# Retention of ten tiles ahead of the main loop, a fixed order of the first loads, and weights joined in PSUM

## The chip, the core and the metric

The program runs on one core of one Trainium2 chip. The core has a matrix engine (PE, with its weight loads shown apart as PEld), a vector engine (DVE), a scalar engine (ACT), a general engine (POOL) and a queue engine (SP) that issues DMAs. Matrix results go to PSUM, which has eight banks of 128 x 512 float32 here; everything else lies in SBUF. The metric is the time of one execution on the chip in microseconds (us): for the kernel before, the median of three runs is 748.28 us (748.04 to 749.37).

## What is computed

Retention over 2304 tokens with 8 heads of 64, and then two MLPs. The weights arrive as float64.

```python
scores = scale * q @ k.T                    # per head, 4 batches of 576 tokens
attn = (scores * gamma ** (i - j))[i >= j] @ v
h = x @ w_in                                # first MLP, 512 -> 1024
solu = h * softmax(h)
ln = (solu - mean) / sqrt(var + 1e-6) * g_ln
x = ln @ w_out                              # 1024 -> 512
h = x @ w_in2                               # second MLP, 512 -> 2048
g = where(h >= 1, h, where(h <= -1, 0, (h + 1) ** 2 / 4))
out = g @ w_out2                            # 2048 -> 512
```

## The kernel before

The tokens are 18 tiles of 128. Retention is recurrent: each tile makes its scores (`ret_scores`, step S: eight matmuls at L116, their product with the decays on DVE at L125, and on POOL the scaling of q, L129, and of k, L132), and its output (`ret_out`, step O: state times q at L144, scores times v at L150, the new state's product at L168, and its addition to the state on DVE at L175 or L181). The output is split into two float32r parts, high and low, on ACT and DVE (L74, L75); every product of the MLPs is three float32r matmuls of such parts.

A weight comes as pairs of 32-bit words and is turned into float32 by `decode`: ACT rescales the high words (L193) and the low words (L194), DVE shifts (L195), POOL adds as integers (L196), and DVE joins the sign (L197, a SCALAR_TENSOR_TENSOR with both its inputs in SBUF). Then ACT writes the high part and DVE or POOL subtracts (L75, for the first MLP's second weight L221 with L223, L224 or L227). Steps A are the four pieces of the first weight `w_in1` (two decodes each), steps B the eight pieces of `w_out1` (one decode each), and `prep_w2` makes the 16 pairs of the second MLP.

What stands ahead of the main loop is written in the string START: L loads a tile of q, k and v, C and G load constants, H is half of a tile's hidden matmuls (L243), N its norm. A step in small letters takes another engine for part of its work. Within START a scheduler places the instructions of all engines, the DMA issues on SP too, by its own estimates; START's steps are only its priorities. After START the matrix engine follows the written order; the other engines are still scheduled. In the main loop, for j = 1 to 8 and a = 2 j, tiles a and a + 1 of the first MLP are worked on, and retention of tiles a + 6 and a + 7 (`LEAD` is 6), until tile 17. With START's S0 to S7 and O0 to O7, the loop begins retention at tile 8.

Loads of q, k and v go through two buffers each (pool `raw`), so the load of a tile waits for the output step of the tile two before it. PSUM has four tags of two banks: `sc` (scores), `o` (retention), `h` (hidden of the first MLP, later projections) and `tr` (transposes). In the second MLP the first block's halves `hidden(0, c)` alternate between `sc` and `tr` for c of 4 and more, and 12 of the 16 weight pairs are prepared while that block runs, after the first MLP's SBUF is free.

Of the kernel before, what the change touches and what calls it, by code (L numbers as in the profile page):

```python
# [24 lines left out]
P = 128  # L25
# [10 lines left out]
START = """  # L36
C1 C0 L0 A0 G0 a1 L1 L2 s0 S1 L3 a2 L4 S2 G1 O0 S3 B0 o1 A3 B1 B2 O2 b3 O3 b4 H0 H1 S4 L5 O4 S5 O5 b5 N0 L6 B6 H2 S6 O6 H3 L7 N1 S7 O7 L8 B7
"""


def shape_constants():
    """The retention's decays, from the shapes alone. Heads are 2 c + e. Within a tile, gamma^(i - j) / sqrt(D)
    from key j to query i >= j; gamma^(i + 1) / sqrt(D) from the row before the tile; gamma^(P - 1 - j) to its
    last row; gamma^P across it."""
    gamma = 1.0 - 2.0 ** (-5.0 - np.arange(H, dtype=np.float64))
    g = gamma.reshape(KD, 2).T
    i = np.arange(P)
# [9 lines left out]
def net(ctx: ExitStack, tc: tile.TileContext, qk_t, kv, w_in1, w_out1, g_ln, w_in2, w_out2, inside, before, after, across, out):  # L57
# [27 lines left out]

# [1 line left out]
    in_sb = at.tile([P, 2, KD, P], F32, name="in_sb", bufs=1)  # L87
# [48 lines left out]
    def ret_out(t, alt=False):  # L136
# [10 lines left out]
        for c in range(KD):  # L147
            for e in range(2):
# [33 lines left out]

# [5 lines left out]
    def decode(st, sp=None):  # L188
# [16 lines left out]
    def prep_w_in1(i, alt=False):  # L205
# [25 lines left out]

# [1 line left out]
    lnT, hps, es = {}, {}, {}  # L233
# [16 lines left out]
    def mlp1_norm(t, alt=False):  # L250
# [78 lines left out]

    def prep_w2(pool, i, sp=None, n0=0):  # L330
# [3 lines left out]
        split(hi.rearrange("p c f -> p (c f)"), lo.rearrange("p c f -> p (c f)"), decode(st, sp))  # L334
# [8 lines left out]
    def split_x2(b):  # L343
# [45 lines left out]

# [1 line left out]
    gs = {}  # L391
# [4 lines left out]
    order = ExitStack()  # L396
    for step in START.split():
        if step[0].islower():
            start[step[0].upper()](int(step[1:]), True)
        else:  # L400
            start[step[0]](int(step[1:]))
    order.enter_context(tc.manual_schedule(engines={nc.tensor.engine}))
# [12 lines left out]
    for j in range(1, NT // 2):  # L415
# [24 lines left out]
        mlp1_hidden(a + 1, 0)  # L440
# [106 lines left out]
```

## Time and profile before

| | |
|---|---|
| median of three runs | 748.28 us |
| the profiled execution, span from first to last instruction | 751.0 us |
| PE busy | 720.1 us (96%) |
| DVE busy | 435.4 us (58%) |
| ACT busy | 285.4 us (38%) |
| POOL busy | 169.8 us (23%) |
| mean granted PE clock | 0.978 |

The trace gives no time of the profiled execution other than its span, so that is its own time here; it is 2.7 us above the median of the runs. Busy time of an engine is the time in which it had an instruction under way; a matmul at a lower granted clock is busy for longer, so busy PE time is not the amount of its work.

### The profile page before, as it was taken

The page shows a single profiled execution, that of the slowest core. Times are in us where ns is not written, and L with a number is a line of the kernel's source. Part 1 is how long each engine was busy: PE and PEld are TensorE (multiplying, and loading weights), DVE is VectorE, ACT ScalarE, POOL GpSimd, SP SyncE. Part 2 cuts the span into 40 slices and gives each one's busy share as a digit, 9 for nine tenths or more (in the row PEclk, how much of TensorE's full clock was granted, in tenths as well). Part 3 has the DMA queues.
Part 4 walks back from the last instruction along what each step waited for, and adds up shares of the span by engine and source line. Part 5 has one row for each costly group of instructions (what it writes and reads, how often), then busy time and mean ns, then how long its engine had stood idle before and what let it go on. Part 6 is the DMA issues. An engine that isn't in the chain of part 4 may idle for free.

```text
span 751.0 us, 10316 instructions
## 1 busy us (share of the span) xinstructions
PE 720.1 (96%) x4096; PEld 606.4 (81%) x4096; DVE 435.4 (58%) x777; ACT 285.4 (38%) x555; POOL 169.8 (23%) x154
## 2 busy tenths in 40 slices
PE   4789999999999999989798999999999999999998
PEld 4678788989888899879676888888888888888896
DVE  4796986574746847685998543344443353434443
ACT  3533663232424635575754322222321242223222
POOL 2785843221211402155654000000000000000000
PEclk9895999999999999999989999999999999999999
DMA  8653543111200301036500010000100001000100
GB/s 342 260 195 115 192 149 110 57 59 55 86 29 1 113 1 57 29 113 211 180 29 28 1 56 1 1 0 1 57 0 1 1 17 40 0 1 1 57 1 28
DMA packets 15183, 50.21 MB, mean 67 GB/s; under 512 B 1952, under 2 KB 2464, under 8 KB 14624
## 3 DMA queue, kind: packets, MB, share of 16 engines
q1 hardware_dynamic: 14848, 49.30, 18.3%
q8 instruction: 32, 0.52, 0.3%
q10 hardware_dynamic: 288, 0.26, 0.1%
q14 instruction: 15, 0.12, 0.1%
HBM read 44.84 MB, written 4.72 MB: 66 GB/s over the span
## 4 chain that ended last, share of the span: by engine, by line
PE 77%; DVE 12%; issue 3%; ACT 3%; POOL 3%; DMA 2%; SPq 0%; POOLq 0%; DVEq 0%; ACTq 0%
PE po L377 23%; PE h L358 23%; PE hp L243 11%; PE px L319 10%; DVE y L197 3%; PE sc L116 2%; DVE y L195 2%; PE po L150 2%; PE pst L168 2%; POOL y L196 2%; DMA st<-in_w_in 2%; PE tp L290 2%; PE po L144 1%; ACT y L193 1%; DVE r L362 1%
## 5 line engine op out<-in xcount | busy, mean ns | idle before, releaser
L377 PE MATMUL po<-wo,gh 128*128 128x512 f32 x576 | 194.1, 398 | 2.7 <-ACT gh L74 2.7
L358 PE MATMUL h<-xsh,wi 128*128 128x512 f32 (+1 forms) x640 | 195.8, 372 | 0.0
L362 DVE SCALAR_TENSOR_TENSOR r<-r 128x512 f32<-128x512 f32 (+1 forms) x80 | 55.6, 695 | 145.6 <-ACT r L361 145.4
L358 PEld LDWEIGHTS h<-xsh,wi 128*128 128x128 f32 x640 | 117.1, 188 | 23.3
L377 PEld LDWEIGHTS po<-wo,gh 128*128 128x128 f32 x576 | 109.2, 190 | 28.9 <-POOL y L196 2.5
L358 PE MATMUL h<-xsl,wi 128*128 128x512 f32 (+1 forms) x320 | 119.0, 372 | 0.0
L377 PE MATMUL po<-wo,gl 128*128 128x512 f32 x288 | 115.1, 400 | 3.8 <-DVE gl L75 3.8
L361 ACT ACTIVATE r<-h 128x512 f32<-128x512 f32 (+1 forms) x80 | 44.3, 554 | 150.6 <-PE h L358 150.1
L243 PE MATMUL hp<-wi1h,x 128*128 128x512 f32 x288 | 91.5, 399 | 0.0
L196 POOL TENSOR_TENSOR y<-y,st 128x512 int32<-128x512 int32 x48 | 67.9, 1418 | 78.0 <-DVE y L195 69.4
L74 ACT ACTIVATE gh<-r 128x512 fp32r<-128x512 f32 (+1 forms) x80 | 47.1, 589 | 95.6 <-DVE r L365 95.6
L319 PE MATMUL px<-lnh,wo1l 128*128 128x256 f32 x288 | 80.8, 281 | 0.0
L319 PE MATMUL px<-lnh,wo1h 128*128 128x256 f32 x288 | 79.7, 277 | 0.0
L319 PE MATMUL px<-lnl,wo1h 128*128 128x256 f32 x288 | 79.7, 277 | 0.0
L75 DVE TENSOR_TENSOR gl<-r,gh 128x512 fp32r<-128x512 f32 (+1 forms) x80 | 55.0, 687 | 42.0 <-ACT gh L74 41.7
L358 PEld LDWEIGHTS h<-xsl,wi 128*128 128x128 f32 x320 | 60.4, 189 | 12.0
L377 PEld LDWEIGHTS po<-wo,gl 128*128 128x128 f32 x288 | 54.6, 190 | 17.5 <-DVE gl L75 5.5
L243 PEld LDWEIGHTS hp<-wi1h,x 128*128 128x128 f32 x288 | 55.3, 192 | 11.9
L243 PE MATMUL hp<-wi1l,x 128*128 128x512 f32 x144 | 60.4, 419 | 3.4 <-DVE wi1l L75 3.3
L197 DVE SCALAR_TENSOR_TENSOR y<-st,y 128x512 uint32<-128x512 uint32 x48 | 49.1, 1024 | 11.1 <-POOL y L196 11.1
L319 PEld LDWEIGHTS px<-lnh,wo1l 128*128 128x128 f32 x288 | 54.1, 188 | 1.3 <-DVE wo1l L227 0.2
L319 PEld LDWEIGHTS px<-lnl,wo1h 128*128 128x128 f32 x288 | 54.1, 188 | 0.2
(73 smaller groups left out, 920.8 us busy)
## 6 DMA issues: line engine op xcount, KB each, us to landing
st<-in_w_out SPq DMA_DIRECT2D x24, 512.0 KB, 3.5
qk<-in_qk_t SPq DMA_DIRECT2D x18, 512.0 KB, 4.3
kv<-in_kv SPq DMA_DIRECT2D x18, 512.0 KB, 3.2
st<-in_w_in SPq DMA_DIRECT2D x16, 512.0 KB, 3.3
st<-in_w_in SPq DMA_DIRECT2D x4, 1024.0 KB, 9.5
out<-osb SPq DMA_DIRECT2D x8, 512.0 KB, 2.8
in_sb<-in_inside SPq DMA_DIRECT2D x2, 256.0 KB, 2.8
bef_sb<-in_before SPq DMA_DIRECT2D x1, 256.0 KB, 8.4
```

The lines of the kernel that those rows point to most:

```text
L74: nc.scalar.activation(hi, src, AF.Copy)
L75: eng.tensor_tensor(out=lo, in0=src, in1=hi.bitcast(F32), op=ALU.subtract)
L116: nc.tensor.matmul(sc[e][:, c, :], qk[rows, 1, c, :], qk[rows, 0, c, :], start=True, stop=True)
L150: nc.tensor.matmul(po[rows, c, :], kv_[:, 1, 2 * c + e, :], probs[t, e][:, c, :], start=(c == 0 and n_in == 0), stop=(c == KD - 1), skip_g ...
L196: nc.gpsimd.tensor_tensor(out=y.bitcast(I32), in0=y.bitcast(I32), in1=lo.bitcast(I32), op=ALU.add)
L197: nc.vector.scalar_tensor_tensor(out=y, in0=hi, scalar=0x80000000, in1=y, op0=ALU.bitwise_and, op1=ALU.bitwise_or)
L243: nc.tensor.matmul(hp, a[:, kk, :], w[:, fs], start=(n == 0), stop=(n == 3 * KD - 1))
L319: nc.tensor.matmul(px[:, mm, :], w[:, ms], a[:, f, :], start=(n == 0), stop=(n == 3 * C1 - 1))
L358: nc.tensor.matmul(hp[:, :n], w[:, kk, :], a[:, :n], start=(i == 0), stop=(i == 3 * KD - 1))
L361: nc.scalar.activation(r[:, :n], hp[:, :n], AF.Relu, bias=0.5, scale=0.5)
L362: nc.vector.scalar_tensor_tensor(out=r[:, :n], in0=r[:, :n], scalar=1.0, in1=r[:, :n], op0=ALU.min, op1=ALU.mult)
L377: nc.tensor.matmul(po[i], a[:, ts_], w, start=(c == 0 and j == 0), stop=(c == C2 - 1 and j == 2))
```

## The change

- START holds the retention of tiles 0 to 9 and loads up to tile 11; in the loop, retention begins at tile 10 (`more = 10 <= ra < NT`), and loads go one tile further ahead. `LEAD` stays 6. The split parts of tiles 0 to 3 lie in buffers of the second MLP's inputs, which are free then.
- SP keeps the order in which START's steps are written (`manual_schedule` on the SP engine). L0 is the first step.
- In `decode`, for the first MLP's weights, ACT writes the rescaled high words to PSUM, and DVE's shift and join read them there; the joined weight stays in PSUM, or goes to SBUF where POOL subtracts. In the second MLP the rescaled words stay in SBUF, and the join writes its result to PSUM. Both splits there run on DVE; before, those of the second weight of a pair ran on POOL.
- Weights take banks of the tags `tr` and `h` (START), `o` (second MLP's pairs 0 to 2) and `tr` (the rest). `hidden(0, c)` of the first block has `sc` alone.
- In the steps B in small letters ACT multiplies by `g` in place of POOL.

```diff
-C1 C0 L0 A0 G0 a1 L1 L2 s0 S1 L3 a2 L4 S2 G1 O0 S3 B0 o1 A3 B1 B2 O2 b3 O3 b4 H0 H1 S4 L5 O4 S5 O5 b5 N0 L6 B6 H2 S6 O6 H3 L7 N1 S7 O7 L8 B7
+L0 C1 C0 G0 L1 s0 A0 G1 O0 S1 L2 o1 A1 L3 S2 o2 A2 L4 S3 A3 O3 L5 S4 B0 O4 L6 S5 b1 O5 L7 B2 S6 O6 H0 H1 L8 b3 S7 O7 N0 L9 B4 S8 O8 b5 H2 H3 L10 S9 O9 N1 B6 b7 L11
...
-        slot = t % LEAD
-        if slot < 2:
+        slot = (t - 4) % LEAD
+        if t < 4:
+            xh, xl = (slab.tile([P, KD, P], F32R, tag=f"xs{w}", name="x1", bufs=4) for w in "hl")
+        elif slot < 2:
...
+    def decode(st, tag, sp=None, sb=False):
...
+        if sp:
+            y = sp.tile([P, 512], U32, tag="y", name="y", bufs=2 if sp is stage else 4)
...
+            w = ps.tile([P, 512], U32, tag=tag, name="w")
+            nc.vector.scalar_tensor_tensor(
+                out=w, in0=hi, scalar=0x80000000, in1=y, op0=ALU.bitwise_and, op1=ALU.bitwise_or
+            )
+            return w.bitcast(F32)
+        w = ps.tile([P, 512], U32, tag=tag, name="w")
+        y = stage.tile([P, 512], U32, tag="y", name="y", bufs=2)
+        nc.scalar.activation(w.bitcast(F32), hi.bitcast(F32), AF.Copy, scale=2.0**-112)
         nc.scalar.activation(lo.bitcast(I32), lo, AF.Copy, scale=2.0**-29)
-        nc.vector.tensor_scalar(y, y, 3, None, op0=ALU.logical_shift_left)
+        nc.vector.tensor_scalar(y, w, 3, None, op0=ALU.logical_shift_left)
         nc.gpsimd.tensor_tensor(out=y.bitcast(I32), in0=y.bitcast(I32), in1=lo.bitcast(I32), op=ALU.add)
+        r = y if sb else w
         nc.vector.scalar_tensor_tensor(
-            out=y, in0=hi, scalar=0x80000000, in1=y, op0=ALU.bitwise_and, op1=ALU.bitwise_or
+            out=r, in0=w, scalar=0x80000000, in1=y, op0=ALU.bitwise_and, op1=ALU.bitwise_or
         )
-        return y.bitcast(F32)
+        return r.bitcast(F32)
...
-            split(hi[:, fs], lo[:, fs], decode(st[:, fs, :]), nc.gpsimd if j and not alt else nc.vector)
+            w = decode(st[:, fs, :], "h" if j else "tr", sb=j)
+            split(hi[:, fs], lo[:, fs], w, nc.gpsimd if j else nc.vector)
...
-        split(hi, lo, decode(st, sp), nc.gpsimd)
+        split(hi, lo, decode(st, tag, sp or stage))
...
-        hp = ps.tile([P, BLK], F32, tag=tag or ("tr" if c % 2 else "sc"), name="h2")
+        hp = ps.tile([P, BLK], F32, tag=tag or ("tr" if c % 2 and b else "sc"), name="h2")
...
+    with tc.manual_schedule(engines={nc.sync.engine}):
+        for step in START.split():
+            start[step[0].upper()](int(step[1:]), *[True] * step[0].islower())
...
-        more = ra < NT
+        more = 10 <= ra < NT
```

How the instructions stand now is shown at three places. The first is SP's queue at the very start. In the kernel before it reads as follows (qk, kv: a tile's q and k, k and v; st: words of a weight; in_sb, aft_sb, bef_sb, acr_sb, g_sb: constants; numbers are buffers).

```order
L96 DMA in_sb_96<-in_inside 128x512 x2
L105 DMA qk_104<-in_qk_t 128x1024
L106 DMA kv_105<-in_kv 128x1024
L207 DMA st_108<-in_w_in1 128x2048
L100 DMA aft_sb_98<-in_after 128x8
L100 DMA bef_sb_97<-in_before 128x512
L207 DMA st_130<-in_w_in1 128x2048
L105 DMA qk_150<-in_qk_t 128x1024
L106 DMA kv_151<-in_kv 128x1024
L207 DMA st_194<-in_w_in1 128x2048
```

In the changed kernel the same place reads so.

```order
L105 DMA qk_104<-in_qk_t 128x1024
L106 DMA kv_105<-in_kv 128x1024
L96 DMA in_sb_96<-in_inside 128x512 x2
L100 DMA aft_sb_98<-in_after 128x8
L100 DMA bef_sb_97<-in_before 128x512
L105 DMA qk_112<-in_qk_t 128x1024
L106 DMA kv_113<-in_kv 128x1024
L222 DMA st_131<-in_w_in1 128x2048
L100 DMA acr_sb_99<-in_across 128x4
L100 DMA g_sb_93<-in_g_ln 128x8
L105 DMA qk_192<-in_qk_t 128x1024
L106 DMA kv_193<-in_kv 128x1024
```

Tile 0's q and k went from the third transfer to the first, and both first tiles stand ahead of the first piece of `w_in1`; of that weight's pieces, three stood among the first twelve issues before and one does now.

The second place is PE where it meets the first hidden matmuls (hp; wi1l, wi1h: the low and high parts of `w_in1`, x1: the split output of tile 0). In the kernel before they follow the scores of tile 1.

```order
L116 MATMUL sc0_173<-qk_150 128x128
L116 MATMUL sc1_174<-qk_150 128x128
L243 MATMUL hp_436<-wi1l0_111,x1_246 128x512
L243 MATMUL hp_436<-wi1h0_110,x1_247 128x512
L243 MATMUL hp_436<-wi1h0_110,x1_246 128x512
L144 MATMUL po_286<-qs_187,state_100 128x128 x4
```

In the changed kernel they follow the scores of tile 7, behind the state product of that tile (po_543).

```order
L150 MATMUL po_483<-p1_464,kv_387 64x128
L116 MATMUL sc1_527<-qk_448 128x128 x4
L144 MATMUL po_543<-qs_540,state_100 128x128 x4
L259 MATMUL hp_569<-wi1l0_134,x1_164 128x512
L259 MATMUL hp_569<-wi1h0_133,x1_165 128x512
L259 MATMUL hp_569<-wi1h0_133,x1_164 128x512
L259 MATMUL hp_569<-wi1l1_227,x1_164 128x512
```

Before, hidden matmuls stood between the retention steps from tile 1 on, a weight piece at a time; now 110 rows of retention alone, of tiles 0 to 7, stand ahead of them.

The third place is DVE in the first block of the second MLP, from the subtraction for one hidden half (gl) to that for the next (r: the activation's steps, h2: the hidden half, y: a weight under way, wi2: its low part). Before:

```order
L75 TENSOR_TENSOR gl_3594<-r_3589,gh_3593 128x512
L197 SCALAR_TENSOR_TENSOR y_3568<-st_3564,y_3568 128x512
L195 TENSOR_SCALAR y_3625<-y_3625 128x512
L362 SCALAR_TENSOR_TENSOR r_3646<-r_3646 128x512
L197 SCALAR_TENSOR_TENSOR y_3613<-st_3609,y_3613 128x512
L195 TENSOR_SCALAR y_3670<-y_3670 128x512
L365 TENSOR_TENSOR r_3646<-h2_3633,r_3646 128x512
L197 SCALAR_TENSOR_TENSOR y_3625<-st_3621,y_3625 128x512
L75 TENSOR_TENSOR wi2_3612<-y_3613,wi2_3611 128x512
L75 TENSOR_TENSOR gl_3651<-r_3646,gh_3650 128x512
```

In the changed kernel (w: a joined weight in PSUM, wo2: the low part of a pair's second weight):

```order
L75 TENSOR_TENSOR gl_3697<-r_3692,gh_3696 128x512
L198 TENSOR_SCALAR y_3611<-y_3611 128x512
L201 SCALAR_TENSOR_TENSOR w_3603<-st_3594,y_3598 128x512
L378 SCALAR_TENSOR_TENSOR r_3751<-r_3751 128x512
L75 TENSOR_TENSOR wo2_3539<-w_3545,wo2_3538 128x512
L198 TENSOR_SCALAR y_3657<-y_3657 128x512
L381 TENSOR_TENSOR r_3751<-h2_3738,r_3751 128x512
L75 TENSOR_TENSOR wi2_3597<-w_3603,wi2_3596 128x512
L201 SCALAR_TENSOR_TENSOR w_3616<-st_3607,y_3611 128x512
L198 TENSOR_SCALAR y_3670<-y_3670 128x512
L75 TENSOR_TENSOR gl_3756<-r_3751,gh_3755 128x512
```

Subtractions of `wo2` stand on DVE now, with their weight operand in PSUM; the joins still read two operands from SBUF.

## Rows read from the trace of the kernel before

**Rows 1.** Windows: length, busy PE, PEld, DVE, ACT, POOL (instructions), PEclk, DMA share, GB/s

```profile
0.00:103.00 103.00, 85.31 (x542) 69.81 (x544) 78.18 (x135) 48.41 (x92) 68.02 (x64) 0.88 0.58 212
103.00:310.00 207.00, 206.83 (x1538) 184.68 (x1536) 126.53 (x294) 84.27 (x190) 46.99 (x53) 1.00 0.17 59
...
348.00:410.00 62.00, 55.52 (x226) 43.18 (x225) 53.81 (x62) 35.37 (x61) 34.13 (x24) 0.94 0.32 113
```

**Rows 2.** PE timeline: the first matmul, and the first output projection

```profile
6.84 2.08 PE L116 MATMUL sc<-qk 64*128 64x128 f32 x16 [6.84 <-DMA qk<-in_qk_t]
...
103.27 0.39 PE L319 MATMUL px<-lnh,wo1l 128*128 128x256 f32 x1
```

**Rows 3.** Chain that ended last, 195 to 440 us: start, us, what

```profile
199.64 1.09 PE sc L116 x16
...
206.39 0.89 PE po L144 x8
207.28 1.02 PE po L150 x16
208.30 1.09 PE pst L168 x8
...
214.85 0.87 PE tp L290 x8
215.73 5.60 PE hp L243 x24
...
415.03 2.80 PE po L377 x12
```

**Rows 4.** Windows of 2 us in the front, columns as in rows 1

```profile
52.00:54.00 2.00, 0.56 (x5) 0.36 (x4) 1.97 (x4) 0.02 (x1) 1.88 (x2) 1.00 0.74 252
58.00:60.00 2.00, 2.00 (x10) 1.78 (x8) 0.56 (x1) 0.83 (x2) 1.92 (x3) 0.50 0.69 250
70.00:72.00 2.00, 2.00 (x10) 1.78 (x9) 0.01 (x1) 0.00 (x0) 1.55 (x2) 0.50 0.35 141
74.00:76.00 2.00, 2.00 (x14) 1.68 (x13) 1.94 (x4) 1.84 (x4) 0.53 (x1) 1.00 0.38 111
```

**Rows 5.** DVE groups, 0 to 103.2 us: count, busy us, mean ns, idle before

```profile
L197 DVE SCALAR_TENSOR_TENSOR y<-st,y 128x512 uint32<-128x512 uint32 x16 | 19.9, 1251 | 1.8 <-POOL y L196 1.8
L195 DVE TENSOR_SCALAR y<-y 128x512 uint32<-128x512 uint32 x17 | 12.0, 711 | 1.6 <-ACT y L193 1.5
L125 DVE TENSOR_TENSOR p<-sc,in_sb 128x512 f32<-128x512 f32 x16 | 10.5, 683 | 9.0 <-PE sc L116 8.1 <-PE po L150 0.8
...
L175 DVE COPY state<-pst 64x256 f32<-64x256 f32 x4 | 1.7, 417 | 0.0
```

**Rows 6.** Durations of the join and the shift over the whole run, min/median/max ns

```profile
L197 DVE SCALAR_TENSOR_TENSOR y<-st,y x48: 674/692/1781, 14.2 to 405.8; 128x512 uint32<-128x512 uint32 x48
...
L195 DVE TENSOR_SCALAR y<-y x48: 407/427/1758, 12.2 to 401.9; 128x512 uint32<-128x512 uint32 x48
```

**Rows 7.** DVE groups, 348 to 410 us

```profile
L197 DVE SCALAR_TENSOR_TENSOR y<-st,y 128x512 uint32<-128x512 uint32 x16 | 16.8, 1049 | 3.8 <-POOL y L196 3.8
L195 DVE TENSOR_SCALAR y<-y 128x512 uint32<-128x512 uint32 x15 | 10.0, 670 | 3.8 <-ACT y L193 3.6
L362 DVE SCALAR_TENSOR_TENSOR r<-r 128x512 f32<-128x512 f32 x8 | 9.1, 1142 | 1.0 <-ACT r L361 1.0
L75 DVE TENSOR_TENSOR wi<-y,wi 128x512 fp32r<-128x512 f32 x8 | 8.9, 1116 | 0.4 <-ACT wi L74 0.4
L75 DVE TENSOR_TENSOR gl<-r,gh 128x512 fp32r<-128x512 f32 x7 | 8.8, 1258 | 0.3
L365 DVE TENSOR_TENSOR r<-h,r 128x512 f32<-128x512 f32 x8 | 5.4, 681 | 0.1
```

**Rows 8.** POOL groups, 348 to 410 us

```profile
L196 POOL TENSOR_TENSOR y<-y,st 128x512 int32<-128x512 int32 x15 | 21.9, 1462 | 17.7 <-DVE y L195 9.5 <-ACT st L194 4.7 <-issue 2.0
L75 POOL TENSOR_TENSOR wo<-y,wo 128x512 fp32r<-128x512 f32 x9 | 13.4, 1493 | 9.0 <-ACT wo L74 9.0
```

More of the change, by code (lines that the diff above doesn't have):

```diff
@@ L186, in words @@
         return src.bitcast(U32).rearrange("p (f t) -> p f t", t=2)
-    def decode(st, sp=None):
+    def decode(st, tag, sp=None, sb=False):
         lo, hi = st[:, :, 0], st[:, :, 1]
-        y = (sp or stage).tile([P, 512], U32, tag="y", name="y", bufs=4 if sp else 2)
-        nc.scalar.activation(y.bitcast(F32), hi.bitcast(F32), AF.Copy, scale=2.0**-112)
+        if sp:
+            y = sp.tile([P, 512], U32, tag="y", name="y", bufs=2 if sp is stage else 4)
+            nc.scalar.activation(y.bitcast(F32), hi.bitcast(F32), AF.Copy, scale=2.0**-112)
+            nc.scalar.activation(lo.bitcast(I32), lo, AF.Copy, scale=2.0**-29)
+            nc.vector.tensor_scalar(y, y, 3, None, op0=ALU.logical_shift_left)
+            nc.gpsimd.tensor_tensor(out=y.bitcast(I32), in0=y.bitcast(I32), in1=lo.bitcast(I32), op=ALU.add)
+            w = ps.tile([P, 512], U32, tag=tag, name="w")
[6 more added lines that the diff above has]
+        nc.scalar.activation(w.bitcast(F32), hi.bitcast(F32), AF.Copy, scale=2.0**-112)
         nc.scalar.activation(lo.bitcast(I32), lo, AF.Copy, scale=2.0**-29)
-        nc.vector.tensor_scalar(y, y, 3, None, op0=ALU.logical_shift_left)
+        nc.vector.tensor_scalar(y, w, 3, None, op0=ALU.logical_shift_left)
         nc.gpsimd.tensor_tensor(out=y.bitcast(I32), in0=y.bitcast(I32), in1=lo.bitcast(I32), op=ALU.add)
+        r = y if sb else w
         nc.vector.scalar_tensor_tensor(
-            out=y, in0=hi, scalar=0x80000000, in1=y, op0=ALU.bitwise_and, op1=ALU.bitwise_or
+            out=r, in0=w, scalar=0x80000000, in1=y, op0=ALU.bitwise_and, op1=ALU.bitwise_or
         )
-        return y.bitcast(F32)
+        return r.bitcast(F32)
     w_in1_sb = [None] * KD
@@ L219, in prep_w_out1 @@
         lo = w1o.tile([P, DM], F32R, name=f"wo1l{f}")
-        y = decode(st)
-        nc.scalar.activation(hi, y, AF.Copy, scale=g_sb[:, f : f + 1])
+        y = decode(st, "h" if alt else "tr", sb=alt)
         if alt:
-            nc.gpsimd.tensor_scalar(y, y, g_sb[:, f : f + 1], None, op0=ALU.mult)
-            nc.gpsimd.tensor_tensor(out=lo, in0=y, in1=hi.bitcast(F32), op=ALU.subtract)
+            nc.scalar.activation(y, y, AF.Copy, scale=g_sb[:, f : f + 1])
+            split(hi, lo, y, nc.gpsimd)
             w_out1_sb[f] = (hi, lo)
             return
+        nc.scalar.activation(hi, y, AF.Copy, scale=g_sb[:, f : f + 1])
         nc.vector.scalar_tensor_tensor(
@@ L328, in net, with prep_w2 @@
     w_in2_sb, w_out2_sb = [None] * C2, [None] * C2
-    def prep_w2(pool, i, sp=None, n0=0):
+    def prep_w2(pool, i, sp=None, n0=0, tag="tr"):
         st = (sp or stage).tile([P, KD * P, 2], U32, tag="st", name="st")
@@ L333, in prep_w2 @@
         hi, lo = (pool.tile([P, KD, P], F32R, tag=f"w{w}{2 * (i - n0)}", name="wi2") for w in "hl")
-        split(hi.rearrange("p c f -> p (c f)"), lo.rearrange("p c f -> p (c f)"), decode(st, sp))
+        split(hi.rearrange("p c f -> p (c f)"), lo.rearrange("p c f -> p (c f)"), decode(st, tag, sp or stage))
         w_in2_sb[i] = (hi, lo)
@@ L396, in net @@
     order = ExitStack()
[L397 to L401, printed above, removed]
+    with tc.manual_schedule(engines={nc.sync.engine}):
+        for step in START.split():
+            start[step[0].upper()](int(step[1:]), *[True] * step[0].islower())
     order.enter_context(tc.manual_schedule(engines={nc.tensor.engine}))
@@ L429, in net @@
             ret_scores(ra)
-        else:
+        elif ra >= NT:
             i = (ra - NT) // 2
             if i == 2:
-                prep_w2(w2a, 2, n0=2)
+                prep_w2(w2a, 2, n0=2, tag="o")
             gs[0, i] = hidden(0, i, "sc")
@@ L438, in net @@
             ret_out(ra)
-            load_qkv(rb)
+            if ra + 2 < NT:
+                load_qkv(ra + 2)
         mlp1_hidden(a + 1, 0)
@@ L447, in net @@
             ret_out(rb)
-            if rb + 1 < NT:
-                load_qkv(rb + 1)
+            if rb + 2 < NT:
+                load_qkv(rb + 2)
         mlp1_out(j - 1, 1)
@@ L454, in net @@
             act2 = ctx.enter_context(tc.tile_pool(name="act2", bufs=3, side="left", reuse_waits="tile"))
-            prep_w2(w2b, 0)
-            prep_w2(w2b, 1)
+            prep_w2(w2b, 0, tag="o")
+            prep_w2(w2b, 1, tag="o")
     prep_w2(w2a, 3, n0=2)
```

## The prediction

> **What bounds the kernel now.** I read the windows by stage first, then the chain of waits, then the timelines and the groups of each engine in the stages that lose time. From 103 to 310 us PE is busy for 206.83 of 207 us at a granted clock of 1.00 [rows 1]; nothing that changes on another engine can help there. Two stages lose time: the front up to 103 us, and the stretch from 348 to 410 us in which the second MLP's weights are prepared. The reader is to see in the windows that PE falls short in these two, and in the groups that DVE is the engine whose time is stretched there.
>
> How much the front loses can be counted. The first output projection starts at 103.27 us [rows 2]. Until then PE has done the scores of ten tiles, the outputs of nine, eight hidden halves and two tiles of transposes. At the steady prices [rows 3] that is 10 x 1.09 (scores), 7.5 x 0.89 (state products: tiles 1 to 8, tile 4 half as wide), 9 x 1.02, 8 x 1.09 (new states), 4 x 5.60 (two hidden halves each) and 2 x 0.87: 59.6 us. So 43.7 us are lost. PE was idle for 103 - 85.3 = 17.7 us [rows 1], 6.84 of them before the first matmul, which waited for tile 0's q and k [rows 2]. The other 26 us are work that ran slower than its steady price, above all at the lower clock: at 58 to 60 and at 70 to 72 us PE was busy all the time and had 0.50, that is 1.2 GHz; before it fell PE had been busy for only 0.56 of 2 us (52 to 54), and at 74 to 76 it has 1.00 again [rows 4]. What ran at 0.50 was retention with three hidden matmuls in it.
>
> **The second MLP's stage.** From 348 to 410 us PE is idle for 62 - 55.5 = 6.5 us, and its clock is 0.94 [rows 1], so up to 3.7 us more; about 9 in all. DVE is busy for 53.8 of 62 us. Its instructions are stretched: the join takes 1049 ns against a median of 692 over the run, the shift 670 against 427 [rows 6, 7], the other two-operand ones in SBUF (L362, the subtractions for wi and gl) 1142, 1116 and 1258, while L365, which reads the hidden half from PSUM, stays at 681 [rows 7]. The stretch is 16 x 0.36 + 15 x 0.24 + 8 x 0.45 + 8 x 0.43 + 7 x 0.57 = 20 us. Over the 15 + 9 POOL instructions of the stage [rows 8] it is 0.85 us for each: whoever reads two operands from SBUF, or runs the fast one-operand shift, waits for POOL.
>
> **The change, part by part.**
>
> *Order of the first loads.* Tile 0's q and k come first; before, the same number of bytes of constants stood ahead. I take 2 us off the 6.84; bounds 0 and 3.5 (half of it). On SP a waiting load now holds all behind it: each L(t) waits for the output step of tile t - 2, and the pieces A1 to A3 and B stand behind such loads. A's are needed at the first hidden matmul, which now stands behind tile 7's scores, so that wait is covered by six tiles of retention; if it isn't, the first hidden half is late by what is missing.
>
> *Ten tiles ahead.* The scores and the product with the state of tile 9 aside, this adds to what stands before the first projection only tile 9's output: 1.02 + 1.09 = 2.1 us, taken from the loop later at the same price. The work up to the projection is then 61.7 us.
>
> *Retention alone on PE, then the hidden halves.* This decides. Scores of tiles 0 to 7 and outputs of 0 to 6 cost 8 x 1.09 + 5.5 x 0.89 + 7 x (1.02 + 1.09) = 28.4 us at full clock and as much again at 1.2 GHz throughout. No row shows so long a stretch of it. Bounds: nothing lost, or 28.4. Before, retention was at 0.50 for the first tiles and for two further stretches, at 1.00 for the rest, so I take two thirds, 18.9.
>
> *Weights joined in PSUM, first MLP.* Sixteen joins took 1251 ns each [rows 5]; with one operand in PSUM I price them as L125, 683 ns, which has its second operand in SBUF and is not stretched: 16 x 0.57 = 9.1 us less on DVE. The shift now reads PSUM too. The nearest row is the copy of half as many columns from PSUM, 417 ns [rows 5], as much as the unhindered shift needs for all 512, 427 ns [rows 6]. I take 0.68 for 16 of them, 10.9 us, against 12.0 before: 1.1 less. Bounds of the shift: 0.43 and 0.71.
>
> The Trainium skill (VectorE: DVE Perf Modes, section Why PSUM operands drop a tier) says that any PSUM operand holds a float32 instruction to one element a cycle, so the shift loses its double rate: a rule against this change. The rows agree as far as a copy shows it. By the rule the shifts cost 10.9 us of DVE; if the double rate survived, 6.8.
>
> Tile 9 adds 2 x 0.68 (L125), 0.68 (its split) and 2 x 0.42 (state) = 2.9 us. DVE's 78.2 us of the front [rows 1] become 78.2 - 9.1 - 1.1 + 2.9 = 70.9. Before, DVE worked from about 9 us on, 83% of the time; at the same share 70.9 us take 85, and end at 93 to 94.
>
> *The front's sum.* 61.7 of work + 18.9 of lower clock + 4.8 before the first matmul + the other idle time as before, 17.7 - 6.8 = 10.9: the first projection starts at 96.3 us. DVE's count says 93 to 94, so neither contradicts the other. Before it would be 103.3 + 2.1 = 105.4 with tile 9's output. Gain: 9.1 us. By the bounds of the clock alone it is 28 or a loss of 0.4.
>
> *Second MLP.* Here the rescaled words stay in SBUF, so the join still reads two operands there and goes on waiting for POOL; only where it writes is new. No row shows DVE writing PSUM; bounds 0.68, what L365 takes with an operand in PSUM, and the 1.05 of now, and I take no change. What gains is the subtraction: wi's weight operand is in PSUM, and its 0.43 of stretch goes. What costs is that nine subtractions come from POOL to DVE: 9 x 0.68 = 6.1 us. POOL keeps 15 instructions of 24, so the stretch falls to 15 x 0.85 = 12.8. DVE: 20.3 to 18.9, or 1.4 less; I take 1 us of it on the path. Bounds: no stretch left, -14 (PE can gain only the 9 it loses), and 15 x (1.781 - 0.692) = 16.3 of stretch [rows 6], +2. The first block's halves have two banks in place of four; I cost that at nothing as long as DVE keeps pace with PE, and see below if not. DVE no longer waits for POOL's subtraction, but the pairs' last step now stands in DVE's own queue, ahead of gl for the projection.
>
> **Sum.** -9 - 1 = -10 us. The profiled execution of 751.0 would be 741.0; the median of the runs is 748.28, so 738.3.
>
> **The rivals.**
>
> *The lower clock holds through the retention.* For: PE was busy all the time at 0.50 for two windows 12 us apart [rows 4], with little but retention on it. Against: in the steady loop retention runs at 1.00 between other matmuls [rows 3]. Then the front costs 61.7 + 28.4 + 4.8 + 10.9 = 105.8: gone. With the second MLP's 1 us, 747; a little less if fewer idle gaps fit in: 746.
>
> *DVE becomes the bound of the second MLP's first block, and the kernel is slower.* Place: 348 to 410 us. For each c DVE has two shifts, two joins, two weight subtractions and three instructions for the half: 2 x 0.43 + 7 x 0.68 = 5.6 us, against PE's 2 x 2.80 = 5.6 [rows 3]. Each POOL add stretches one of them by up to 1.09 us, two for each c: 7.8. Twelve c's take 94 us in place of 67, 27 more, of which 9 are there already: +18, and with two banks PE can't run ahead. With the front's -9 it is +9: 757. It decides from (67 + 9 + 9) / 12 = 7.1 us for a c. For: DVE at 87% now. Against: POOL has two instructions for each c in place of three.
>
> *Weights hold the banks of the hidden halves.* Four of the B's occupy tag h in START through shift, add and join, at least 0.68 + 1.46 + 0.68 = 2.8 us each; while one does, two halves can't both be under way. If each delays PE in full, with as much again for the queues, 4 x 5.6 = 22 us come in place of part of the 10.9: the front then takes 107.8, +2.4, total 750.
>
> **How the numbers follow.** Forecast, 738.3 (731 to 744): 0.52. Clock rival: 0.22. DVE rival: 0.14. Bank rival: 0.12. A measurement of this kernel tells about 0.2%, 1.5 us, from no change. Faster: 0.52 x 0.95 + 0.22 x 0.65 + 0.14 x 0.1 + 0.12 x 0.15 = 0.67. Same: 0.08. Slower: 0.25. The range goes from 726 (lower clock for a third in place of two thirds, -9.5, and 3 us more in the second MLP) to 753, between the bank and the DVE rival.
>
> **What would show it.** The first matmul near 4.8 us; the first projection near 96 us; joins of the first MLP at 0.68 us and shifts at 0.68; joins of the second still above 0.9; windows of 20 to 60 us with clock at 0.5 for more than half. Wrong, if PE's stretch of retention is at 1.00 (then the gain is larger), if the first projection comes after 105 us, or if PE's idle time from 340 to 410 us exceeds 15 us.

## Result and the profile after

The changed kernel takes 742.77 us (median of 15 runs, 741.12 to 747.28), the kernel before 748.67 in the same series: ratio 0.9919, 95% interval [0.9898, 0.994], or 5.9 us less. The forecast was 738.3, 10 us less. The profiled execution has a span of 745.1 us against 751.0, again 5.9 less. The time came out near the forecast, but by luck: the gain came from the wrong stretches, and two errors of opposite sign nearly cancelled. The front was to give 9 of the 10 us and gave about none, the second MLP was to give 1 and gave nearly all.

Windows of the kernel after, by the stages of [rows 1] (columns as there):

```profile
0.00:103.00 103.00, 80.27 (x555) 65.77 (x556) 72.17 (x139) 54.81 (x104) 63.90 (x66) 0.90 0.62 228
103.00:310.00 207.00, 205.48 (x1511) 183.75 (x1510) 121.14 (x285) 78.55 (x179) 36.85 (x44) 1.00 0.14 47
310.00:348.00 38.00, 38.00 (x277) 35.40 (x276) 24.93 (x53) 21.66 (x45) 8.29 (x7) 1.00 0.21 72
348.00:410.00 62.00, 57.38 (x240) 44.13 (x239) 58.65 (x83) 41.54 (x75) 28.70 (x20) 1.00 0.45 152
```

And the one stage of the kernel before that [rows 1] left out:

```profile
310.00:348.00 38.00, 34.99 (x256) 32.16 (x254) 32.85 (x58) 25.87 (x51) 20.68 (x16) 1.00 0.32 107
```

From 310 to 348 us PE's 3.0 us of idle time are gone; I had put nothing on that stage. From 348 to 410 us the clock rose from 0.94 to 1.00. In the front PE is idle for 22.7 of 103 us in place of 17.7. PE's timeline of the kernel after (start, us, what, in brackets the wait ahead of it), to be read beside [rows 2], shows where:

```profile
4.64 2.08 PE L116 MATMUL sc<-qk 64*128 64x128 f32 x16 [4.64 <-DMA qk<-in_qk_t]
9.72 0.69 PE L150 MATMUL po<-p,kv 128*64 128x128 f32 x2 [3.01 <-DVE p L125]
...
80.96 0.50 PE L259 MATMUL hp<-wi1l,x 128*128 128x512 f32 x1 [1.43 <-DVE y L212]
...
88.17 0.50 PE L259 MATMUL hp<-wi1l,x 128*128 128x512 f32 x1 [3.70 <-DVE e L275]
...
98.91 0.69 PE L259 MATMUL hp<-wi1l,x 128*128 128x512 f32 x1 [2.45 <-DVE e L275]
...
106.15 0.28 PE L335 MATMUL px<-lnh,wo1l 128*128 128x256 f32 x1
```

The first output projection starts at 106.15 us. With tile 9's output (2.1 us) it would be 105.4 in the kernel before [rows 2], so in these two executions the front lost 0.8 us. This place moves from one execution to the next: with this front it lies at 100.84 to 106.15 us in five traces (the kernel after, e1, e2, e5 and e6 below), with the old front at 102.94 to 104.04 in three (before, e3, e9). That the front alone is worth nothing therefore rests on the times of e1 and e3, not on the 0.8. What follows takes 639.0 us in place of 647.7; less the 2.1 that moved, 6.7 us were gained there.

The front was ahead at 80 us. What PE still had to do from there to the projection, in the kernel after and then before (groups: count, busy us, mean ns, idle before):

```profile
L259 PE MATMUL hp<-wi1h,x 128*128 128x512 f32 x40 | 14.8, 455 | 0.0
L259 PE MATMUL hp<-wi1l,x 128*128 128x512 f32 x20 | 9.6, 479 | 7.6 <-DVE e L275 6.2 <-DVE y L212 1.4
L306 PE MATMUL tp<-ident,e 128*128 128x128 f32 x12 | 1.6, 272 | 0.0
```

```profile
L243 PE MATMUL hp<-wi1h,x 128*128 128x512 f32 x36 | 11.3, 394 | 0.0
L243 PE MATMUL hp<-wi1l,x 128*128 128x512 f32 x17 | 6.9, 407 | 0.0
L150 PE MATMUL po<-p,kv 128*64 128x128 f32 x32 | 2.5, 280 | 0.0
L116 PE MATMUL sc<-qk 64*128 64x128 f32 x32 | 2.3, 285 | 0.0
L290 PE MATMUL tp<-ident,e 128*128 128x128 f32 x16 | 2.3, 276 | 1.5 <-DVE e L275 1.3 <-DVE sm L254 0.2
L144 PE MATMUL po<-qs,state 128*128 128x128 f32 x16 | 2.1, 275 | 0.0
L168 PE MATMUL pst<-kv 128*128 128x128 f32 x8 | 1.2, 288 | 0.0
```

At the prices of [rows 3] that is 15.3 us of work after (60 x 0.233 + 12 x 0.109) and 21.2 before, of 61.7 and 59.6 in all. So at 80 us the changed kernel was 46.4 - 38.4 = 8 us of work ahead. It then took 26.15 us for its 15.3, the kernel before 23.27 for its 21.2: of the 8.8 us given back, 5.7 are idle time (7.1 against 1.5) and 3.1 slower matmuls (the clock from 80 us on was 0.87 against 1.00). Before, retention of tiles 7 and 8 stood between the hidden halves; now only transposes do. A half waits until the norm of the tile before it (L275) has read the two banks of `h`.

DVE's joins and shifts in the front, answering to [rows 5], and the groups of 348 to 410 us, answering to [rows 7, 8]:

```profile
L209 DVE TENSOR_SCALAR y<-w 128x512 uint32<-128x512 uint32 x16 | 10.9, 685 | 0.9 <-POOL wi1l L75 0.7
...
L212 DVE SCALAR_TENSOR_TENSOR w<-w,y 128x512 uint32<-128x512 uint32 x8 | 5.6, 694 | 1.2 <-POOL y L210 1.1
L212 DVE SCALAR_TENSOR_TENSOR y<-w,y 128x512 uint32<-128x512 uint32 x8 | 5.5, 686 | 2.8 <-POOL y L210 2.8
```

```profile
L199 POOL TENSOR_TENSOR y<-y,st 128x512 int32<-128x512 int32 x20 | 29.6, 1483 | 32.8 <-DVE y L198 21.1 <-ACT wo L74 2.8 <-ACT st L197 2.8
...
L201 DVE SCALAR_TENSOR_TENSOR w<-st,y 128x512 uint32<-128x512 uint32 x20 | 18.2, 920 | 0.0
...
L198 DVE TENSOR_SCALAR y<-y 128x512 uint32<-128x512 uint32 x19 | 10.6, 564 | 1.5 <-ACT y L196 1.5
L75 DVE TENSOR_TENSOR gl<-r,gh 128x512 fp32r<-128x512 f32 x8 | 9.3, 1167 | 0.0
L378 DVE SCALAR_TENSOR_TENSOR r<-r 128x512 f32<-128x512 f32 x9 | 8.3, 924 | 0.3 <-ACT r L377 0.3
...
L75 DVE TENSOR_TENSOR wo<-w,wo 128x512 fp32r<-128x512 f32 x10 | 6.8, 680 | 1.7 <-ACT wo L74 1.7
L75 DVE TENSOR_TENSOR wi<-w,wi 128x512 fp32r<-128x512 f32 x9 | 6.1, 679 | 0.4 <-ACT wi L74 0.4
```

Whatever reads one operand from PSUM takes 0.68 to 0.69 us; what reads two from SBUF is stretched as before. The Trainium skill (SBUF — State Buffer, section Who interferes with whom) says that a DVE instruction with two SBUF inputs contends with a POOL instruction that reads SBUF, and one with at most one does not, outside the doubled-rate modes. These rows agree: 0.68 for the weight subtractions, 0.92 to 1.17 for the others.

### The profile page after: what moved, and what is told of

Its sections match the earlier page's. It is cut to its first block, busy times and chain, and to the rows that moved or that the text cites. A ratio compares the mean times of both kernels' runs of the same rounds, so it can differ in the third digit from the quotient of the medians.

```text
span 745.1 us, 10361 instructions
## 1 busy us (share of the span) xinstructions
PE 712.7 (96%) x4096; PEld 601.1 (81%) x4096; DVE 420.3 (56%) x790; ACT 287.4 (39%) x563; POOL 137.7 (18%) x136
## 4 chain that ended last, share of the span: by engine, by line
PE 79%; DVE 8%; DMA 5%; issue 3%; ACT 2%; POOL 1%; SPq 0%; DVEq 0%; ACTq 0%; POOLq 0%
PE po L393 23%; PE h L374 23%; PE hp L259 12%; PE px L335 10%; PE po L150 3%; PE sc L116 3%; DMA st<-in_w_out 2%; DMA st<-in_w_in 2%; PE pst L170 2%; DVE w L201 2%; PE tp L306 2%; PE po L144 1%; DVE gl L75 1%; DVE y L198 1%; DMA aft_sb<-in_after 1%
## 5 line engine op out<-in xcount | busy, mean ns | idle before, releaser
L378 DVE SCALAR_TENSOR_TENSOR r<-r 128x512 f32<-128x512 f32 (+1 forms) x80 | 53.2, 665 | 142.9 <-ACT r L377 142.8
L259 PE MATMUL hp<-wi1h,x 128*128 128x512 f32 x288 | 94.3, 410 | 0.0
L259 PEld LDWEIGHTS hp<-wi1h,x 128*128 128x128 f32 x288 | 57.2, 199 | 12.9
L199 POOL TENSOR_TENSOR y<-y,st 128x512 int32<-128x512 int32 x32 | 46.5, 1458 | 67.1 <-DVE y L198 34.5
L335 PEld LDWEIGHTS px<-lnh,wo1h 128*128 128x128 f32 x288 | 54.2, 188 | 0.0
```

Of the source, the lines that this page charges most:

```text
L259: nc.tensor.matmul(hp, a[:, kk, :], w[:, fs], start=(n == 0), stop=(n == 3 * KD - 1))
L335: nc.tensor.matmul(px[:, mm, :], w[:, ms], a[:, f, :], start=(n == 0), stop=(n == 3 * C1 - 1))
L378: nc.vector.scalar_tensor_tensor(out=r[:, :n], in0=r[:, :n], scalar=1.0, in1=r[:, :n], op0=ALU.min, op1=ALU.mult)
```

## The experiments

All ratios are to the kernel before, run on the same chip in the same series; the changed kernel's is 0.9919.

**1 and 2. Undo the second MLP's part; undo the buffers' rotation.** In the diffs `decode2` is `decode` of the kernel before; for `wi` it is put in likewise, with the subtraction on DVE.

```diff
-        split(hi, lo, decode(st, tag, sp or stage))
+        split(hi, lo, decode2(st, sp), nc.gpsimd)
-        hp = ps.tile([P, BLK], F32, tag=tag or ("tr" if c % 2 and b else "sc"), name="h2")
+        hp = ps.tile([P, BLK], F32, tag=tag or ("tr" if c % 2 else "sc"), name="h2")
```

> The changed kernel, with the second MLP's weights and hidden banks as before: joins in SBUF, the second weight of a pair subtracted on POOL, hidden halves alternating between sc and tr; the front and the rotated x1 buffers stay. Theory (the whole gain was made between 328 and 418 us, 3.4 of it before 346 and 3.9 behind, and the latter is the work of the second MLP's joins and subtractions): the 3.9 are lost, ratio to before 0.997; the first projection stays near 106 us; DVE's joins of 348 to 410 us are stretched again to about 1.05 us. If the waits of the transposes near 331 to 335 us come back too, 1.001. Rival (the gain comes from the front, and the second MLP is worth the 1 us that was forecast): ratio 0.993.

Measured: 750.74 us, ratio 1.0031 [1.0, 1.0063]. The whole gain goes and a little more, which is beyond both expectations: the second MLP's part is worth 0.0112, about 8 us, and the new front with the rotation none.

```diff
-        slot = (t - 4) % LEAD
+        slot = t % LEAD
```

> The changed kernel with one line undone: the split output of tile t (of 4 and more) lies in buffer t % 6 again in place of (t - 4) % 6, so tiles 16 and 17 hold the buffers that the weights of pair 3 need. Theory (the 3.4 us between 328 and 346 come from pairs 2 and 3 being prepared earlier, because their buffers come free with tiles 12 and 13 and not 16 and 17): the transposes wait for DVE at 331 to 337 us again, 3 us or so, ratio to before 0.996. Rival (the PSUM joins free DVE there): no change against the changed kernel, 0.992.

Measured: 742.81 us, ratio 0.9917 [0.9888, 0.9947]; no transpose waits between 310 and 348 us. My theory fell: with the other edits in place the rotation is worth nothing.

**3. The second MLP's part alone, with the rotation, in the kernel before.** The edits are those of the change in `prep_w2`, in `decode` for its weights (here `decode2`), in `hidden` and in the tags of the pairs.

```diff
-        slot = t % LEAD
+        slot = (t - 4) % LEAD
...
-        split(hi, lo, decode(st, sp), nc.gpsimd)
+        split(hi, lo, decode2(st, tag, sp or stage))
...
-        hp = ps.tile([P, BLK], F32, tag=tag or ("tr" if c % 2 else "sc"), name="h2")
+        hp = ps.tile([P, BLK], F32, tag=tag or ("tr" if c % 2 and b else "sc"), name="h2")
```

> The kernel before with only the second MLP's part of the change (joins into PSUM, all subtractions on DVE, hidden halves of the first block in sc, tags of the pairs) and the rotated x1 buffers; START, the first MLP's weights and ten tiles ahead are not in it. Theory (the front of the change is worth about nothing, +0.8 us): as fast as the changed kernel or 1 us faster, ratio to before 0.990 to 0.992, first projection near 103.3 us. Rival (the front carries the gain): 0.998 to 1.000.

Measured: 740.51 us, ratio 0.9879 [0.9836, 0.9923], first projection at 102.94 us. Without the new front the kernel is no slower than with it; the intervals overlap, so whether the front costs 3 us or nothing isn't told.

**5, 6 and 9. What in the second MLP gains: PSUM, or POOL's subtractions?** e5_sub_dve is e1_mlp2_old with one argument taken out, e9_one_word is the same edit in the kernel before, and e6_wo_pool is the changed kernel with `wo` joined in SBUF and subtracted on POOL. First the edit of e5, then that of e6:

```diff
-        split(hi, lo, decode2(st, sp), nc.gpsimd)
+        split(hi, lo, decode2(st, sp))
```

```diff
-            w = ps.tile([P, 512], U32, tag=tag, name="w")
+            w = y if sb else ps.tile([P, 512], U32, tag=tag, name="w")
...
-        split(hi, lo, decode(st, tag, sp or stage))
+        split(hi, lo, decode(st, tag, sp or stage, True), nc.gpsimd)
```

> As e1_mlp2_old (the changed front, the second MLP's weights as before), but the second weight of each pair is subtracted on DVE in place of POOL; joins and subtractions read and write SBUF, no weight goes through PSUM. Theory (the gain of the second MLP is that DVE's instructions on weights have an operand in PSUM and so don't wait for POOL; to take the subtractions from POOL alone isn't worth it): the subtractions of wo cost DVE 0.7 to 1.4 us each, PE waits for gl as long as in e1_mlp2_old or longer, ratio to before 1.000 to 1.008. Rival (the gain is that POOL has 9 instructions less in 348 to 410 us and the rest is not stretched any more): ratio 0.993.

Measured: 742.47 us, ratio 0.9917 [0.9886, 0.9948]. The rival won: with no weight of the second MLP in PSUM the time is that of the changed kernel. Its hidden halves alternate over four banks, the changed kernel's over two; what each of the two is worth alone isn't separated.

> The changed kernel, but the second weight of each pair is joined in SBUF and subtracted on POOL, as before; the first weight of a pair is joined in PSUM and subtracted on DVE, as in the changed kernel, and the banks are as there. Theory (operand in PSUM): half of the gain stays, since the subtractions of wi (1.38 us in e1_mlp2_old from 348 to 410 us) fall to 0.68; ratio 0.995 to 0.998. Rival (fewer POOL instructions): the gain goes, 1.001 to 1.004.

Measured: 754.39 us, ratio 1.0074 [1.0045, 1.0104], worse than both expected. With POOL subtracting, a PSUM operand for half of the weights did not bring the gain. That it does harm isn't shown: this run also keeps two banks for the hidden halves where e1 has four.

> The kernel before with one argument taken out: the second weight of each pair of the second MLP is subtracted on DVE, as the first one, and not on POOL. Nothing else of the change is in it. Theory (the gain of the change is this edit alone, as e5_sub_dve against e1_mlp2_old says: 8 us): ratio to before 0.987 to 0.991, DVE's waits of 331 to 337 us and the 10 us lost by PE from 348 to 410 us mostly gone, first projection near 103.3 us. Rival (it takes the rotated buffers or the changed front as well): 0.995 to 1.000.

Measured: 749.16 us, ratio 0.9991 [0.9964, 1.0019]. The one edit isn't enough in the kernel before.

The windows of 364 to 382 us, in which each kernel loses most, are in this order: before, after, e1, e6, e5, and e9 with the window behind it. The same work lies up to 6 us earlier or later from one to the other.

```profile
364.00:382.00 18.00, 14.00 (x49) 10.65 (x48) 17.64 (x20) 11.65 (x21) 12.40 (x8) 0.81 0.34 120
```

```profile
364.00:382.00 18.00, 14.96 (x63) 11.17 (x62) 17.59 (x26) 12.45 (x23) 8.19 (x6) 1.00 0.62 186
```

```profile
364.00:382.00 18.00, 13.67 (x46) 10.09 (x45) 17.97 (x19) 10.46 (x18) 12.05 (x9) 0.81 0.26 90
```

```profile
364.00:382.00 18.00, 11.89 (x43) 8.81 (x42) 17.96 (x20) 13.14 (x23) 14.60 (x10) 0.88 0.42 146
```

```profile
364.00:382.00 18.00, 14.66 (x55) 11.12 (x55) 17.90 (x25) 10.65 (x19) 6.63 (x4) 0.91 0.18 58
```

```profile
364.00:382.00 18.00, 12.26 (x50) 8.79 (x48) 18.00 (x24) 12.48 (x22) 8.92 (x7) 0.99 0.34 117
382.00:400.00 18.00, 16.49 (x61) 13.23 (x62) 16.17 (x25) 10.10 (x17) 5.51 (x4) 0.82 0.09 30
```

DVE is full in all six. With POOL busy for 12 to 15 us it finishes 19 or 20 instructions, of 0.88 to 0.95 us each (17.64 / 20, 17.97 / 19); with POOL busy for 7 to 9 us it finishes 24 to 26, of 0.68 to 0.75. So, as these windows read, the subtractions taken from POOL pay by shortening what is left on DVE. PE then gets more done: in the kernel after 63 matmuls in place of 49, and 14 x 0.233 is 3.3 us of work. Of that 1.0 us is less idle time (3.0 in place of 4.0); the other 2.3 us come with a clock of 1.00 in place of 0.81. In e9 DVE has the better pace, but PE still waited 2.14 and 2.83 us close together, and the clock was at 0.82 in the window behind:

```profile
380.18 0.50 PE L377 MATMUL po<-wo,gh 128*128 128x512 f32 x1 [2.14 <-ACT gh L74]
383.51 0.80 PE L377 MATMUL po<-wo,gl 128*128 128x512 f32 x1 [2.83 <-DVE gl L75]
```

Over the whole stretch from 348 to 410 us e9's PE did 223 matmuls, the kernel before 226, the kernel after 240, e5 245. What e9 lacks beside e5 is the rotation and the new front; no run has the one without the other, so which of them makes the edit pay stays open. e2 shows only that with the joins in PSUM the rotation isn't needed.

**4 and 7. The banks of the hidden halves.**

```diff
-        hp = ps.tile([P, 512], F32, tag="h", name="hp")
+        hp = ps.tile([P, 512], F32, tag="o" if t == 2 else "h", name="hp")
...
-        mlp1_transpose(a - 1)
+        if j > 1:
+            mlp1_transpose(a - 1)
...
         mlp1_norm(a + 1)
+        if j == 1:
+            mlp1_transpose(a - 1)
```

> The changed kernel with tile 2's two hidden halves in the banks o, which retention has left by then, in place of h, and the transposes of tile 1 behind tile 3's halves. Theory (the front was 8 us ahead at 80 us and gave it back because hidden halves of tiles 2 and 3 wait for the norm of the tile before them to leave the two banks of h, with no retention left in between to cover it): the waits of 3.70 us at 88.2 and 2.45 us at 98.9 go, the first projection comes at 100 to 102 us, ratio to before 0.984 to 0.987. Rival (late weights and a full DVE and ACT keep PE back there, the banks only show it): PE waits for DVE or ACT elsewhere before the first projection, which stays within 1 us of 106; ratio 0.992.

Measured: 734.66 us, ratio 0.9816 [0.9776, 0.9856]: 8 us less than the changed kernel and more than either expectation. PE no longer waits for L275 ahead of the projection, which comes at 93 us:

```profile
93.00 0.38 PE L335 MATMUL px<-lnh,wo1l 128*128 128x256 f32 x1 [2.22 <-DVE lnl L75]
```

Part of that is a clock of 0.98 to 80 us in this execution against 0.91. e2, whose front is the changed kernel's, had 0.98 too and its projection at 100.84: against it the projection is 7.8 us earlier, of which the two waits were 6.1.

> Tile 2's hidden halves in the banks o as in e4_banks_o, but the transposes of tile 1 stay ahead of tile 3's halves. Theory (the norm's latency is what is uncovered, 4 us from a half's last matmul to the end of L275 and 10 us to the normalized tile): hidden halves no longer wait, and the transposes of tile 1 wait for its norm (L291) instead, 3 to 4 us; ratio 0.986 to 0.989, between the changed kernel and e4_banks_o. Rival (only the two banks matter): as e4_banks_o, 0.982.

Measured: 739.09 us, ratio 0.987 [0.9839, 0.9901], as the theory said; of the waits (us in total, times, longest) one is

```profile
PE tp L306 <- DVE e L291: 3.7, 1, 3.7
```

The norm is what has no cover; banks alone take away one of the two waits and move the other to the transposes.

**8. The start.** One letter in START, on top of e4_banks_o:

```diff
-L0 C1 C0 G0 L1 s0 A0 G1 O0
+L0 C1 C0 G0 L1 S0 A0 G1 O0
```

> e4_banks_o with tile 0's kv scaled on POOL in place of DVE (s0 becomes S0), so that DVE's queue no longer begins with an instruction that waits for aft_sb until 8.3 us. Theory (the 2.2 us that the first matmul gained were lost to this wait of 3.0 us): the first output of retention starts at 7.4 to 8.5 us in place of 9.7, and the time falls by 1 to 2 us, ratio 0.979 to 0.981. Rival (from 14 to 34 us PE waits for DVE and the loads anyway, with DVE busy 17.8 of 20 us and the DMA engines 0.94): the start is earlier, the first projection isn't, ratio 0.9816 as e4_banks_o.

Measured: 731.89 us, ratio 0.9769 [0.9737, 0.9801], the fastest kernel here. DVE's first rows in the changed kernel, and then e8's:

```profile
8.38 0.69 DVE L132 TENSOR_TENSOR kv<-kv,aft_sb 128x512 f32<-128x512 f32 x1 [7.52 <-DMA aft_sb<-in_after]
8.99 1.28 DVE L125 TENSOR_TENSOR p<-sc,in_sb 128x512 f32<-128x512 f32 x2
```

```profile
7.59 1.29 DVE L125 TENSOR_TENSOR p<-sc,in_sb 128x512 f32<-128x512 f32 x2 [6.74 <-DMA in_sb<-in_inside]
```

The product with the decays starts 1.4 us earlier, and 0.9 earlier than e4's 8.46. The first output started at 8.34 us (e4 9.20), the projection at 90.51, 2.5 before e4's, and the time is 2.8 less. The direction is the theory's; the size is not its 1 to 2 us, and the intervals overlap. The 0.9 us at the start don't account for 2.5 at the projection: the clock from 34 to 52 us was 1.00 here and 0.93 in e4, so how much the edit itself is worth isn't told.

**10 and 12. The first MLP's weights, on top of e8.** e10 gives tag `tr` to all of them; e12 decodes them in SBUF as before (its lines stand behind the #).

```diff
-            w = decode(st[:, fs, :], "h" if j else "tr", sb=j)
+            w = decode(st[:, fs, :], "tr", sb=j)         # e12: decode2(st[:, fs, :])
-        y = decode(st, "h" if alt else "tr", sb=alt)
+        y = decode(st, "tr", sb=alt)                     # e12: decode2(st)
```

> e8_kv_on_pool, with all weights of the first MLP in the two banks of tag tr while they are decoded; in the changed kernel half of them take a bank of h, the tag of the hidden halves. Theory (the banks that weights take in h cost the 2.4 to 2.9 us that hidden halves wait for L212, and no more): ratio 0.974 to 0.977, first projection 1 to 3 us earlier than in e8_kv_on_pool. Rival (two banks are too few for sixteen weights: DVE, ACT and POOL then wait for one another, and the weights come late): ratio 0.980 to 0.990.

Measured: 740.16 us, ratio 0.9882 [0.9855, 0.9908]. The rival won: the first transposes now wait for the weights.

```profile
PE tp L306 <- DVE wo1l L243: 12.3, 1, 12.3
```

> e8_kv_on_pool with the first MLP's weights decoded as before: rescaled, shifted and joined in SBUF, no weight in a PSUM bank before the main loop; the order of START stays. Theory (the PSUM operand takes 0.57 us off each of sixteen joins, 9 us of DVE, and DVE is busy 18.6 of 20 us from 14 to 34 us): joins near 1.2 us again, first projection 2 to 5 us later, ratio 0.980 to 0.984. Rival (DVE has room, and what weights do in the banks of h costs as much): ratio 0.974 to 0.978.

Measured: 741.49 us, ratio 0.9917 [0.9889, 0.9946]. With the norm covered, decoding the first MLP in PSUM is worth 9.6 us, where 2 to 5 were expected; part of that is the clock, 0.93 to 80 us against 1.00 in e8. The projection comes at 101.94 us in place of 90.51, and the joins up to 90 us read

```profile
L224 DVE SCALAR_TENSOR_TENSOR y<-st,y 128x512 uint32<-128x512 uint32 x14 | 15.8, 1131 | 0.3 <-POOL y L223 0.3
```

**11. e8 with the second MLP of e5.**

```diff
-        split(hi, lo, decode(st, tag, sp or stage))
+        split(hi, lo, decode2(st, sp))
```

> e8_kv_on_pool with the second MLP's weights as in e5_sub_dve: joined in SBUF, both subtractions on DVE, hidden halves of the first block alternating between sc and tr. Theory (joining the second MLP's weights in PSUM is worth nothing once POOL has the adds alone): the same time as e8_kv_on_pool within 1 us, ratio 0.976 to 0.978. Rival (the PSUM operand helps by itself, and e5_sub_dve was as fast only by its four banks for hidden halves): 0.980 or more.

Measured: 735.41 us, ratio 0.982 [0.9791, 0.985], 3.5 us more than e8. That looks like the rival, but the loss isn't where most of the edit is. In the two traces e11 is 6.8 us longer, and 6.4 of them are there when the last projection of the first MLP begins (335.8 against 329.4 us). From 90 to 100 us, first e8 and then e11 have

```profile
90.00:100.00 10.00, 9.49 (x83) 9.49 (x84) 6.13 (x19) 4.89 (x14) 2.27 (x3) 1.00 0.01 2
```

```profile
90.00:100.00 10.00, 6.74 (x45) 6.50 (x43) 8.34 (x28) 7.20 (x17) 2.92 (x4) 0.83 0.21 72
```

DVE does 28 instructions there in place of 19, one of them a join for the second MLP (L224): the scheduler placed that work differently. As a test of PSUM in the second MLP this run is inconclusive; e5 is the one to go by.

## Why the prediction was right in sum and wrong in its parts

*The first loads.* Right for PE's first matmul (4.64, forecast 4.8), but the 2.2 us gained were given back at once: DVE's queue began with the scaling of `kv`, which waited for `aft_sb` until 8.38 us, so the first output started at 9.72 us, against 9.70 before the change. I had followed SP's queue and not the one behind it; in e8 the first output comes 0.9 us earlier than in e4.

*DVE in the front.* Right: joins 0.69 and shifts 0.685 us, busy 72.2 us in place of the forecast 70.9. The Trainium skill's rule on float32 from PSUM (VectorE: DVE Perf Modes, section Why PSUM operands drop a tier) held for this uint32 shift too: 685 ns against 427 [rows 6].

*The lower clock, 18.9 us.* Near in size by luck, wrong in its place. PE was busy for 83.4 us up to the projection (80.27, and the 3.15 behind 103 us), 21.7 above the 61.7 of work; in e2, with the same front, 78.6 us, or 16.9 above it. But retention alone did not run at 0.5, as these windows of the kernel after show:

```profile
14.00:34.00 20.00, 16.32 (x175) 13.90 (x176) 17.77 (x32) 15.68 (x32) 15.51 (x16) 1.00 0.94 356
34.00:52.00 18.00, 15.81 (x107) 13.19 (x105) 13.66 (x23) 8.22 (x14) 17.69 (x18) 0.81 0.62 222
52.00:68.00 16.00, 14.36 (x118) 11.92 (x118) 12.45 (x27) 7.64 (x16) 9.20 (x9) 1.00 0.53 190
68.00:80.00 12.00, 11.54 (x65) 9.00 (x63) 9.39 (x16) 6.63 (x12) 7.06 (x7) 0.72 0.64 231
```

By the prices of [rows 3], an estimate, about 13 of the 21.7 us lie in the windows of 34 to 52 us, 68 to 80 and 80 to 106, whose clock is below 0.9. About 3 lie in the first 14 us, where the first sixteen score matmuls took 2.08 us and not 1.09 although the record shows 1.00. The rest lies in windows at 1.00, where PE had work in hand but took longer than the steady price. The forecast's own sign of a larger gain, retention at 1.00, came in part, and its sign of being wrong, a projection after 105 us, came with it.

*The front's idle time: the step that failed.* "The other idle time as before, 17.7 - 6.8 = 10.9" was 18.1 (22.7 - 4.6). That, with 2.8 of slower work, is the distance from 96.3 to 106.15 us. PE's two largest waits up to 107 us, in the kernel after, are (us in total, times, longest)

```profile
PE hp L259 <- DVE e L275: 6.2, 2, 3.7
PE po L150 <- DVE p L125: 5.9, 4, 3.0
```

For the first instruction PE waited 1.3 us before the change. I moved away the retention that had stood behind the hidden halves of tiles 1 and 2 and covered their norms, and did not ask what covers them now. 6.2 us of waits came of it, and e4 and e7 show that they are the norm's. The second wait was 0.8 us before; 3.0 of the 5.9 are the first output's, told above. In turn the 3.3 us that hidden matmuls had waited for the subtractions of `w_in1` are gone. The bank rival came near (the front +0.8 in place of its +2.4), but by the norm in the banks of `h`; the weights there held halves for 1.8 us in two waits.

*The second MLP, -1 us: mis-sized.* It was about -8 (e1 against the changed kernel), -6.7 in the two traces. The sum over DVE came out. The stretch left is 20 x 0.23 + 19 x 0.14 + 8 x 0.49 + 9 x 0.24 = 13 us (forecast 12.8, though over 15 POOL instructions and not the 20 of this window), the subtractions 10 x 0.68 = 6.8 (forecast 6.1), and joins were at 0.92. But DVE's busy time over a stage isn't what PE waits for. I counted nothing for 310 to 348 us, where 3.0 us of waits went, and nothing for the clock, 2.3 us from 364 to 382; the idle time itself fell by only 1 us in that window (4.0 to 3.0).

*The DVE rival* asked for 7.1 us for each c; from 348 to 410 us there are three waits for L381, 3.7 us together, and 0.9 us for `gl`, against 6.5 us of idle time before.

## What to carry to other kernels

Before work is moved out of a stretch, name what latency it was covering there: retention taken from between the first hidden halves left a norm of 4 us bare twice, and the waits of 6.2 us used up most of the 8 us that the move had gained. When two engines slow each other, look at how many instructions the full one finishes in the window that loses time, not at its busy time. And look at the head of every queue that waits for the transfers, not only at the one that issues them.

## What the runs showed of the hardware

The mean granted clock of one and the same program differed between executions: 0.984 to 0.993 over the 15 of the changed kernel. In e7 it stood at 0.76 from 34 to 52 us, in e8 at 1.00. The rows say what PE did before: in e7 it had been busy for 0.61 of 2 us when the clock fell to 0.50, that is 1.2 GHz, in e8 for 1.47 at the same place. A busy PE did not bring the clock back at once: e7's was busy throughout from 34 to 42 us at 0.50. First e7, then e8:

```profile
30.00:32.00 2.00, 0.61 (x8) 0.49 (x5) 1.99 (x4) 0.73 (x2) 2.00 (x5) 1.00 0.98 369
34.00:36.00 2.00, 2.00 (x16) 1.67 (x13) 1.37 (x3) 1.19 (x3) 2.00 (x3) 0.50 0.37 147
40.00:42.00 2.00, 2.00 (x11) 2.00 (x11) 1.80 (x4) 0.60 (x1) 2.00 (x3) 0.50 0.95 373
```

```profile
30.00:32.00 2.00, 1.47 (x10) 1.12 (x10) 1.94 (x5) 1.08 (x2) 2.00 (x4) 1.00 0.83 279
```

No run varies this alone, so the cause of the difference stays open. A join that writes PSUM takes as long as one that writes SBUF: 683 ns at the least and 692 in the median over 32 of the changed kernel, against 674 and 692 [rows 6].
